# A per-pack table of planner choices, and a second side bank late, in a fused attention and GLU kernel

## The chip, the cores and the metric

One core of a Trainium2 chip runs the whole program. The metric is the device time of one execution in microseconds (us); the median of several executions is compared. A kernel is planned in Python when it is built, so on the chip every engine follows a fixed list of instructions with waits on semaphores.

The engines are called PE (matrix products; PEld is its weight load), DVE (vector), ACT (scalar, with the exp and gelu tables), POOL (GpSimd) and SP (issues DMAs).

## The reference

For x of 2048 rows and 640 columns in bf16, with 32 heads of 20 columns that share one key and one value head:

```python
q = (LN(x) @ wq) as 32 heads of 20;  k = LN(x) @ wk;  v = LN(x) @ wv
p = softmax(q k^T / sqrt(20))              # 32 x 2048 x 2048 scores
h = x + (p v, heads side by side) @ wo
g = LN(h) @ w_gate;  u = LN(h) @ w_up      # 640 -> 1536
out = h + (gelu(g) * u) @ w_down
```

LN is a layer norm without weights; gelu is the tanh form.

## The kernel before, in words

**Tiles and units.** The rows are 16 tiles of 128. The queries are taken in nine chunks (`CHUNKS`): seven of two tiles and two of one tile (tiles 14 and 15). A chunk's 32 heads make four units for two tiles, or two units for one tile; there are 32 units. Each unit meets the 16 key tiles, so there are 32 x 16 = 512 *packs*. A pack is four score matmuls of 128 x 512 in four PSUM banks (L1306), one for each row group of the PE array. `state["npack"]` counts the packs that have been issued; it is the key of every per-pack choice and ends at 512.

**Exp on two engines.** A score tile is turned into its exponential on ACT (L1688, one bank alone or two adjoining banks in one instruction) or on DVE. DVE writes an integer whose bits are a rough exponential (L1782), and two shifted copies of it refine the result; these are made by POOL (L1756 for one tile, L1738 for both shifts of one) or by DVE (L1732). A DVE tile so needs three value products on PE (L1390) where an ACT tile needs one. The value products of a unit gather in an accumulation bank, 6 or 7.

**Banks.** Scores use banks 0 to 5. Banks 6 and 7 hold the accumulation of the open unit and one side product at a time; when neither is in use they may take scores. A *side product* is any other work of PE: queries, wo, gate, up and down products, and transposes on PE. It is a `_Job` of several pieces, with a bank of its own from its first piece until another engine has emptied it (L609 while scores run, L605 afterwards).

**The planner.** A forward loop takes the engine that is free earliest, by estimated costs, and asks its function (`pe_decide`, `act_decide`, ...) for the next instruction. For PE the order is: a pack if four score banks are free; half a pack (two rows) if two are free and the estimate finds it worth while (`HALF_ON and light(t) and ...`); else value products, a piece of a side product or a filler matmul on zeros (L1529), each only if it ends before `lim`, the estimated time of the next pack. `issue_qk` chooses how many tiles of a whole pack go to DVE from DVE's backlog (usually one), and `issue_half` does so for each half. `next_piece` picks the side product and its bank: `pool_b` is [7, 6], with banks 5 and 4 while keys are being made (`head`) and all six others once all scores are issued (`tail`).

**Choices by hand.** `tw(kind, d)` looks up `TWEAK[(kind, npack)]` and otherwise returns the planner's own value `d`. Its kinds are "n" (DVE tiles of a whole pack), "a" and "b" (those of the first and the second half), "h" (split the pack or not), "l" (ns added to `lim`), "m" (no side product now) and "t" (three banks in one exp). In the kernel before `TWEAK` is empty.

**The end of the work.** `PE_T2` lists the tiles whose normalised rows of the second layer norm are transposed on PE (five transposes and a copy) rather than by a DMA of SP; `PE_TO` and `PE_ON` do so for other transposes. Gate products are emptied by DVE (L960) and go through gelu on ACT later (L987) while exps remain, and go straight through gelu (L962) after the last exp. Up products are multiplied in by DVE (L1004). The down products are added to the rows by DVE (L1022), and SP stores the tile.

Of the kernel before, what the change touches and what calls it, by code (L numbers as in the profile page):

```python
# [219 lines left out]
def bass_sequential_preLN__grouped_kv_mqa__glu_gated_geglu__prompt_kernel(  # L220
# [37 lines left out]
    PH = (8, 99)  # L258
    PE_T1 = (0, 1)
    LN_POOL = (2, 4, 6, 8)  # L260
    PE_T2 = (15,)
    PE_TO = (15,)
    PE_ON = (30, 31)
    POOL_NM = 750.0
# [94 lines left out]
    def c_act(n):  # L359
        return n / 1.2 + 51.0  # L360
# [11 lines left out]
    PVF = 99  # L372
# [15 lines left out]
    LOCKW = 200.0  # L388
    YIELD = 700.0
    WQA = 1  # L390
    TWEAK = {}
    T_LAT = (1700.0, 2700.0, 2700.0)
    ADDW = 60.0
    MISCMAX = 1500.0
# [39 lines left out]
    active = []  # L434
    sp_tasks = []
    state = {"mode": "m", "tab": "exp", "npack": 0, "exps_left": 2048, "misc_ready": False, "kv_left": NT, "qk_left": 512, "half": None}
# [28 lines left out]
    def ln_group(ln, tiles, prio, done):  # L465
# [38 lines left out]
        def norm(t):  # L504
# [9 lines left out]
            def then(op):  # L514
# [14 lines left out]

                if t in (PE_T1 if ln == 0 else PE_T2):  # L530
                    tr_job(("tr", ln, t), xn_tmp[:, s, :], ("xt", s), o, wkeys, lambda: slots["xt"].append(s),
# [83 lines left out]
    def tr_job(name, src, key, o, wkeys, sent, done):  # L615

        pieces = []
        for c in range(NC_D):
            pieces.append(((lambda c: lambda e, b, mode: e.transpose(
                psb[:, b * 1024 + c * P:b * 1024 + (c + 1) * P], src[:, c * P:(c + 1) * P], ident[:]))(c),  # L620
                "t", [key, "ident"]))

        def then(b):
            sent()

            def fin(op):
                free_bank(b)
                done(op)
            flex_copy(o, psb[:, b * 1024:b * 1024 + D].rearrange("p (c n) -> p c n", c=NC_D), D, [("b", b)], wkeys,
                      0.1, fin)  # L630
        jobs.append(_Job(name, 0.1, pieces, then))
# [481 lines left out]
    def open_units():  # L1113
        return [u for u in units if u["npk"] > 0 and not u["evac"]]

    def next_pack(t):
        nopen = 0
        for u in units:
            if u["evac"]:
                continue  # L1120
            if u["npk"] > 0:
                nopen += 1
            if u["left"]:
                if u["npk"] == 0 and nopen >= 2:
                    return None
                if u["qop"] is None or u["qop"].vis > t + 20:
                    return None
                for kt in u["left"]:
                    op = key_ready.get(kt)
                    if op is not None and op.vis <= t + 20:  # L1130
                        return u, kt
                if u["npk"] == 0:
                    return None
            if nopen >= 2:
                return None
        return None
# [18 lines left out]
    def free_banks(t):  # L1155
        res = []
        for b in score_banks():
            if bank_owner[b] is None:
                res.append((plan.ready("pe", (), [("b", b)]), b))
        return sorted(b for r, b in res if r <= t + 30), res  # L1160
# [23 lines left out]
    def tw(kind, d):  # L1184

        return TWEAK.get((kind, state["npack"]), d)

# [245 lines left out]
    def pe_decide(t):  # L1433
        half = state["half"]
        cand = half or next_pack(t)
        piece = None if tw("m", 0) else next_piece(t)
        state["misc_ready"] = piece is not None
        ok, allb = free_banks(t)
        if half is not None:
            if len(ok) >= 2:  # L1440
                issue_half(t, half[0], half[1], half[2], ok, None)
                return True
        elif cand and len(ok) >= 4:
            issue_qk(t, cand[0], cand[1], ok)
            return True

        tq = 1e12
        if cand:
            est = [x[0] for x in allb]
            ta = plan.free["act"]  # L1450
            for kind, tl in act_q:
                ta = max(ta, tl[0]["vis"]) + c_act(512 * len(tl))
                est += [ta + L_ACT] * len(tl)
            td = plan.free["dve"]
            for x in dve_q:
                td = max(td, x["vis"]) + 600
                est.append(td + L_DVE)
            est.sort()
            tq = est[3] if len(est) > 3 else 1e12
            if half is not None:  # L1460
                tq = est[1] if len(est) > 1 else 1e12
            elif len(ok) >= 2 and state["npack"] > HBEG and state["tab"] == "exp" and tw(
                    "h", HALF_ON and light(t) and tq + 445.0 - act_end() > HGAIN):
                k = state["npack"]
                state["nhalf"] = state.get("nhalf", 0) + 1
                issue_half(t, cand[0], cand[1], [k % 4, (k + 1) % 4], ok, [(k + 2) % 4, (k + 3) % 4])
                return True
        lim = max(tq, act_end() - 570.0) + tw("l", 0.0)
        qs = pv_rounds(t)
        full = min(len(q) for q in qs)  # L1470
        most = max(len(q) for q in qs)
        flush = any(u["closed"] for u in open_units())
        nr = full if not flush else most
        press = pa_free.count(True) < PRA or pd_free.count(True) < PRD
        if press and nr == 0:
            nr = min(most, 1)
        def fits(c):
            return t + c <= lim

        def do_pv():  # L1480
            sw = pe_sw(t, "v")
            k = 1
            issue_pv(t, qs, k)
            return True

        def do_piece():
            jb, pc = piece
            issue_piece(t, jb, pc)
            return True

        swv = pe_sw(t, "v")
        can_v = nr >= 1 and (fits(216.0 + swv) or press)
        can_m = piece is not None and fits(c_pe(piece[1][1], "v") + (
            pe_sw(t, "m") if piece[1][1] == "t" else swv))
        if can_v and (press or state["qk_left"] == 0):
            return do_pv()
        if can_m and piece[0].prio < 1.0:
            return do_piece()
        if can_v and nr >= PVF:
            return do_pv()  # L1500
        if can_m:
            return do_piece()
        if can_v:
            return do_pv()
        if fits(222.0 + swv) and quiet(t):
            return fill(t)
        return False
# [30 lines left out]
    def next_piece(t):  # L1538
        for jb in active:
            pc = jb.pieces[jb.pos]  # L1540
            if plan.ready("pe", pc[2], [("b", jb.bank)]) <= t + 20:
                return jb, pc
        if len(active) >= 2:
            return None
        banks = []
        need_acc = any(u["acc"] is None for u in open_units()) and not (
            state["kv_left"] == 0 and any(bank_owner[b] is not None and bank_owner[b][0] == "acc" for b in (6, 7)))
        head = state["kv_left"] > 0
        tail = state["qk_left"] == 0
        pool_b = [7, 6]  # L1550
        if head and state["npack"] < HEADN:
            pool_b += [5, 4] if state["npack"] < HEAD2 else [5]
        if tail:
            pool_b += [5, 4, 3, 2, 1, 0]
        for b in pool_b:
            if bank_owner[b] is None:
                banks.append(b)
        fixed = [b for b in banks if b in (6, 7)]
        if need_acc and len(fixed) <= 1 and fixed:
            banks = [b for b in banks if b not in (6, 7)]  # L1560
        if not banks:
            return None
        cur = min([u["id"] for u in units if u["left"]] or [99])
        best = None
        for jb in jobs:
            pr = jb.prio
            if jb.name[0] == "q":
                ahead = jb.name[1] - cur
                pr = 0.2 if ahead <= 0 else (0.9 if ahead <= 1 else 8.0 + 0.01 * ahead)
            elif jb.name[0] == "qd":  # L1570
                pr = 0.5 if jb.name[1] - cur <= QAHEAD + 1 else QPRI + 0.01 * jb.name[1]
            if best is not None and pr >= best[0]:
                continue
            if jb.gate is not None and not jb.gate():
                continue
            if any(k not in plan.w for k in jb.pieces[0][2]):
                continue
            for b in banks:
                if plan.ready("pe", jb.pieces[0][2], [("b", b)]) <= t + 20:
                    best = (pr, jb, b)  # L1580
                    break
        if best is None:
            return None
        jb = best[1]
        return _Start(jb, best[2]), jb.pieces[0]
# [311 lines left out]
    while True:  # L1897
# [6 lines left out]
        if eng in ("pe", "dve", "act"):  # L1904
# [10 lines left out]
            k = (int(t // 100000), eng, why)  # L1915
# [85 lines left out]
```

The softmax here doesn't subtract the row's maximum and nothing guards it: scores larger than these inputs give would overflow.

## Time and profile before

| what | value |
|---|---|
| median of 8 executions | 772.97 us (771.25 to 775.39) |
| profiled execution | 771.25 us, span of its instructions 769.5 us |
| mean granted clock of PE | 0.998 |
| score tiles: on DVE, on ACT | 630, 1418 |
| start of pack 25, of pack 460, of pack 511 | 55.4, 663.5, 738.7 us |
| last exp on ACT ends | 740.9 us |

Times in the tables are counted from the start of the span. A row of a group gives the line, engine, operation and shapes, the count after x, then the time that the group was busy and the mean length of one, then how long the engine had been idle before these instructions and what ended that. A wait row gives who waited for whom: the sum in us, how often, and the longest. A pack's start is that of its first score matmul, counted off in fours from the 2048 in the trace.

### The profile page before, as it was taken

The numbers are of one execution on the slowest core, as the hardware profiler recorded it, in microseconds if no ns is written. First come the engines' busy times: TensorE is split into PE (matmuls) and PEld (weight loads), VectorE is DVE, ScalarE is ACT, GpSimd is POOL, SyncE is SP. The second block draws the span as 40 slices with busy tenths as digits, with TensorE's granted clock in tenths as the row PEclk, the third lists the DMA queues.
The fourth block names the chain that finished last, engine by engine and source line by source line (L and its number), as shares of the span: only waits on it lengthen the run. The fifth ranks groups of instructions, "written<-read, shape, count | busy, mean of one in ns | idle before, by whom it ended". The sixth has DMA issues, their size and how long they took to land.

```text
span 769.5 us, 29575 instructions
## 1 busy us (share of the span) xinstructions
PE 710.3 (92%) x12946; PEld 336.0 (44%) x12946; DVE 611.7 (80%) x1113; ACT 726.2 (94%) x1086; POOL 659.7 (86%) x721
## 2 busy tenths in 40 slices
PE   4788899999889899999999899999899999989998
PEld 3332223342334455445334444455444544434567
DVE  8878888888988767878788777878788786888853
ACT  5899999999999999999999999999999999999961
POOL 5698998999999888989999987879898998998740
PEclk9999999999999999999999999999999999999999
DMA  7543421000110001100101001010011000211000
GB/s 209 97 126 86 109 62 26 20 9 9 26 26 9 10 12 35 26 26 10 24 11 26 3 10 44 9 43 10 4 35 35 9 10 12 35 26 18 12 19 19
DMA packets 56768, 25.88 MB, mean 34 GB/s; under 512 B 47808, under 2 KB 55360, under 8 KB 56640
## 3 DMA queue, kind: packets, MB, share of 16 engines
q1 hardware_dynamic: 55328, 23.55, 13.5%
q8 instruction: 103, 1.69, 0.9%
q10 hardware_dynamic: 1312, 0.44, 0.2%
q14 instruction: 25, 0.20, 0.1%
HBM read 10.21 MB, written 2.62 MB: 17 GB/s over the span
## 4 chain that ended last, share of the span: by engine, by line
PE 55%; ACT 32%; DVE 8%; DMA 3%; issue 1%; POOL 0%; DVEq 0%
ACT pa L1688 31%; PE ps L609 21%; PE ps L1390 16%; PE ps L1306 14%; DVE pd L1782 5%; PE ps L605 3%; DMA xn1T<-xn_tmp 1%; DVE osb L1417 1%; DMA xh<-in_A_x_dram 1%; ACT gbuf L987 1%; PE ps L1529 1%; DVE gbuf L1004 1%; DMA onr<-osb 1%; DVE qT L679 0%; ACT L1688 0%
## 5 line engine op out<-in xcount | busy, mean ns | idle before, releaser
L1688 ACT ACTIVATE pa<-ps 128x512 bf16<-128x512 f32 (+1 forms) x1038 | 680.6, 815 | 12.0 <-PE ps L1306 6.7
L1756 POOL TENSOR_TENSOR pd<-pd,shifts 128x512 int32<-128x512 int32 x564 | 574.7, 1040 | 64.9 <-DVE pd L1782 60.5
L1782 DVE TENSOR_SCALAR pd<-ps 128x512 uint16<-128x512 f32 x630 | 417.8, 687 | 121.1 <-PE ps L1306 111.0
L1390 PE MATMUL ps<-pd,v_ext 128*32 128x512 bf16 x1890 | 291.2, 383 | 13.8 <-DVE osb L1417 7.0
L1390 PE MATMUL ps<-pa,v_ext 128*32 128x512 bf16 x1418 | 265.9, 384 | 2.8 <-ACT pa L1688 1.7
L1306 PE MATMUL ps<-qT,kT 32*128 32x512 bf16 x2048 | 221.7, 384 | 27.7 <-DVE pd L1782 10.6
L1306 PEld LDWEIGHTS ps<-qT,kT 32*128 32x128 bf16 x2048 | 61.2, 91 | 201.5 <-DVE pd L1782 107.6
L1390 PEld LDWEIGHTS ps<-pd,v_ext 128*32 128x32 bf16 x1890 | 80.4, 95 | 78.0 <-issue 41.9
L1390 PEld LDWEIGHTS ps<-pa,v_ext 128*32 128x32 bf16 x1418 | 71.0, 95 | 41.8 <-issue 27.2
L609 PE MATMUL ps<-xn2T,wu_sb 128*32 128x256 bf16 x1680 | 67.0, 274 | 2.1 <-DVE qT L679 1.4
L609 PE MATMUL ps<-xn2T,wg_sb 128*32 128x256 bf16 x1680 | 66.3, 274 | 0.0
L609 PE MATMUL ps<-wd_sb,gbuf 128*32 128x320 bf16 x1264 | 59.2, 301 | 0.0
L609 PE MATMUL ps<-xn1T,wq_pad 128*32 128x256 bf16 (+1 forms) x1440 | 52.2, 266 | 0.7 <-ACT pa L1688 0.6
L609 PEld LDWEIGHTS ps<-xn2T,wu_sb 128*32 128x32 bf16 x1680 | 42.9, 96 | 20.2 <-issue 9.7
L609 PEld LDWEIGHTS ps<-xn2T,wg_sb 128*32 128x32 bf16 x1680 | 41.5, 96 | 18.5 <-issue 12.0
L1738 POOL TENSOR_TENSOR pd<-pd,shifts 128x256 int32<-128x256 int32 x64 | 42.8, 687 | 0.0
L609 PEld LDWEIGHTS ps<-wd_sb,gbuf 128*32 128x32 bf16 x1264 | 31.6, 96 | 20.9 <-issue 9.7
L1004 DVE TENSOR_TENSOR gbuf<-ps,gbuf 128x512 bf16<-128x512 f32 x48 | 32.9, 685 | 9.6 <-PE ps L605 5.0
L609 PEld LDWEIGHTS ps<-xn1T,wq_pad 128*32 128x32 bf16 x1440 | 33.5, 97 | 14.5 <-issue 8.4
L462 DVE BATCH_NORM_STATS2 stats<-xh 128x6 f32<-128x320 bf16 x64 | 29.9, 476 | 1.5 <-DMA xh<-in_A_x_dram 1.0
L609 PE MATMUL ps<-wo_sb,onT 128*32 128x320 bf16 x600 | 29.7, 301 | 0.0
L960 DVE CAST gbuf<-ps 128x512 bf16<-128x512 f32 x42 | 28.8, 686 | 0.3
(76 smaller groups left out, 355.1 us busy)
## 6 DMA issues: line engine op xcount, KB each, us to landing
out_dram<-xh SPq DMA_DIRECT2D x16, 160.0 KB, 1.8
xh<-in_A_x_dram SPq DMA_DIRECT2D x3, 640.0 KB, 6.5
wd_sb<-in_B_w_down_dram SPq DMA_DIRECT2D x4, 480.0 KB, 3.7
wg_sb<-in_B_w_gate_dram SPq DMA_DIRECT2D x2, 576.0 KB, 5.3
wu_sb<-in_B_w_up_dram SPq DMA_DIRECT2D x2, 576.0 KB, 5.6
wg_sb<-in_B_w_gate_dram SPq DMA_DIRECT2D x2, 384.0 KB, 4.1
wu_sb<-in_B_w_up_dram SPq DMA_DIRECT2D x2, 384.0 KB, 4.4
wo_sb<-in_A_wo_dram SPq DMA_DIRECT2D x1, 480.0 KB, 3.5
```

The source lines that it names most:

```text
L462: dve(lambda e: e.bn_stats(stats[:, ln, t, 6 * h:6 * h + 6], xh[:, t, h * HALF:(h + 1) * HALF]), 395, [key], [("st", ln, t, h)], prio, c)
L605: return e.matmul(o(b), l, r, start=st, stop=sp)
L609: ins = e.matmul(o(b)[a, :], l[:, a], r, start=st, stop=sp, tile_position=(0, 32 * j))
L960: dve(lambda e: e.tensor_copy(o, i), c_dve(n * k), [("b", bk)], ks, 1.0, fin)
L987: task(("act",), (lambda v: lambda e: e.activation(v, v, ACT.Gelu_apprx_tanh))(v), ("gelu", c_act(n * (f1 - f0))), L_ACT, ks, ks, 1.0, (la ...
L1004: dve(lambda e: e.tensor_tensor(o, i, o, ALU.mult), c_dve(n * k), [("b", bk)] + ks, ks, 1.0, fin)
L1306: ins = e.matmul(bank(b), kT4[32 * r:32 * r + 32, kt * P:(kt + 1) * P], qT[32 * r:32 * r + 32, s, :], start=True, stop=True, tile_position ...
L1390: ins = e.matmul(ps[32 * r:32 * r + 32, ab * 512:(ab + 1) * 512], v_ext[:, it["kt"], it["w"], :], it["ap"], start=st, stop=(j in ends), ti ...
L1688: op = plan.commit("act", lambda e: e.activation(dst, src, ACT.Exp, scale=SM_SCALE), cost, L_ACT, [("b", b0 + db * i) for i in range(n)], ...
L1738: return e.tensor_tensor(pd32[:, w, h], pd32[:, 0, h], shifts[:, w - 1:w].to_broadcast([P, 256 * k]), ALU.add)
L1756: return e.tensor_tensor(pd32[:, 1:3, h], pd32[:, 0, h].unsqueeze(1).to_broadcast([P, 2, 256 * k]), shifts[:].unsqueeze(2).to_broadcast([P ...
L1782: op = plan.commit("dve", lambda e: e.tensor_scalar(pd[:, 0, s * 512:(s + 1) * 512], bank(b), CH_A, CH_B, ALU.mult, ALU.add), c_dve(512), ...
```

## The change

Four things change. `TWEAK` is filled from a table with 132 entries, by kind and pack number. A new kind "v" lets value products go ahead of side products in a pack. From pack 460 on, and while fewer than two side products are active, a side product may take bank 5 as well as 6 and 7. And the second layer norm of tile 14, not of tile 15 alone, is transposed on PE. The branch with `PVF` was not reached before, since `PVF` is 99; `next_piece` returned nothing before too when two side products were active, so `LACT = 2` sets no further limit.

```diff
-    PE_T2 = (15,)
+    PE_T2 = (14, 15)
...
-    TWEAK = {}
+
+    TABLE = {
+        "a": {27: 1, 28: 1, 44: 1, 127: 1, 140: 0, 142: 0, 171: 0, 295: 1, 369: 1, 379: 0, 434: 1, 441: 1,
+             464: 1},
+        "b": {29: 0, 78: 1, 96: 0, 125: 0, 203: 1, 301: 0, 345: 0, 395: 1, 426: 1, 428: 1, 432: 0, 446: 1,
+             504: 1, 523: 0},
+        "h": {42: 1, 72: 0, 80: 0, 95: 1, 115: 1, 194: 0, 215: 0, 223: 0, 236: 1, 270: 1, 283: 1, 287: 1,
+             324: 0, 347: 0, 349: 1, 350: 0, 358: 1, 374: 1, 382: 0, 432: 0, 467: 0, 471: 1},
+        "l": {26: -200.0, 35: 150.0, 98: -200.0, 106: -100.0, 124: -200.0, 131: 150.0, 136: 300.0, 158: 300.0,
+             208: 150.0, 211: -400.0, 221: -200.0, 240: 300.0, 272: 300.0, 280: -200.0, 294: 300.0, 304: 150.0,
+             308: -200.0, 310: -100.0, 333: -100.0, 335: -100.0, 346: 300.0, 368: -100.0, 370: -200.0,
+             395: -400.0, 408: -200.0, 409: 300.0, 423: -100.0, 439: 300.0, 449: -200.0, 477: 300.0,
+             479: -200.0, 482: 150.0, 484: 150.0, 488: -100.0, 495: 150.0, 506: -100.0, 511: 150.0,
+             526: -400.0},
+        "m": {107: 1, 119: 1, 305: 1, 335: 1, 449: 1, 519: 1},
+        "n": {27: 0, 35: 2, 72: 2, 137: 2, 176: 1, 195: 1, 207: 1, 244: 0, 287: 1, 326: 1, 347: 1, 366: 1,
+             408: 1, 417: 2, 441: 1, 447: 0, 478: 2, 487: 1, 511: 0, 518: 0, 523: 1, 525: 0},
+        "v": {25: 1, 33: 1, 90: 1, 138: 1, 139: 1, 142: 1, 155: 1, 192: 1, 210: 1, 253: 1, 256: 1, 281: 1,
+             358: 1, 359: 1, 505: 1, 514: 1, 519: 1},
+    }
+    TWEAK = {(kind, k): v for kind, row in TABLE.items() for k, v in row.items()}
+    LATE = 460
+    LACT = 2
...
-        if can_v and nr >= PVF:
+        if can_v and (nr >= PVF or tw("v", 0)):
             return do_pv()
...
         if tail:
             pool_b += [5, 4, 3, 2, 1, 0]
+        elif state["npack"] >= LATE and len(active) < LACT:
+            pool_b += [5]
```

## The prediction

> **What bounds the kernel now.** I read the engine shares first, then the busy time by stretch, then the groups of instructions, the waits of the score stage, and the order of instructions at the end.
>
> ```profile
> PE 710.3 (92%) x12946; PEld 336.0 (44%) x12946; DVE 611.7 (80%) x1113; ACT 726.2 (94%) x1086; POOL 659.7 (86%) x721
> ```
> ```profile
> 0.00:60.00 60.00, 43.70 (x776) 20.32 (x776) 48.12 (x142) 47.16 (x75) 44.78 (x82) 0.97 0.59 141
> 60.00:740.00 680.00, 639.96 (x11834) 293.48 (x11831) 552.19 (x948) 671.88 (x1004) 613.35 (x639) 1.00 0.11 25
> 740.00:769.50 29.50, 26.64 (x346) 22.22 (x343) 11.43 (x24) 7.19 (x10) 1.57 (x2) 1.00 0.07 24
> ```
>
> The columns after the length are PE, PEld, DVE, ACT, POOL. In the 680 us of the score stage ACT is busy 671.88 us, so 8.1 us are left to it; DVE has 127.8 us and POOL 66.7 us idle. ACT sets the rate there. PE looks full, but it runs 324 filler matmuls on the zero tile (28.7 us), which the planner issues only when PE has been slack.
>
> ```profile
> L1756 POOL TENSOR_TENSOR pd<-pd,shifts 128x512 int32<-128x512 int32 x564 | 574.7, 1040 | 64.9 <-DVE pd L1782 60.5 <-DVE ln_ve L480 0.4 <-DVE ln_vb L480 0.4
> L1782 DVE TENSOR_SCALAR pd<-ps 128x512 uint16<-128x512 f32 x630 | 417.8, 687 | 121.1 <-PE ps L1306 111.0
> L1688 ACT ACTIVATE pa<-ps 128x1024 bf16<-128x1024 f32 x380 | 407.3, 1078 | 2.3 <-PE ps L1306 2.0
> L1688 ACT ACTIVATE pa<-ps 128x512 bf16<-128x512 f32 x658 | 390.7, 664 | 9.8 <-PE ps L1306 4.7
> ```
>
> Of 2048 score tiles 630 go to DVE (1.23 per pack of four) and 1418 to ACT, 760 in pairs and 658 alone. The means include an overlap with the next instruction: the median distance between starts of back-to-back ones is 904 ns for a pair, 478 ns for a single and 607 ns for a DVE tile. These spacings are the prices below.
>
> ```profile
> DVE pd L1782 <- PE ps L1306: 105.4, 179, 1.2
> PEld ps L1306 <- DVE pd L1782: 104.0, 304, 1.1
> PEld ps L1306 <- ACT pa L1688: 48.7, 109, 0.9
> ACT pa L1688 <- PE ps L1306: 2.8, 13, 0.4
> ```
>
> These waits are of 60 to 740 us. Scores wait for banks that ACT and DVE must empty; DVE waits for scores; ACT waits for almost nothing.
>
> At the end the chain is another. The last exp ends at 740.9, and the order of instructions shows:
>
> ```profile
> 741.80 0.69 DVE L1417 CAST osb<-ps 128x512 bf16<-128x512 f32 x1 [1.91 <-PE ps L1390]
> ...
> 752.35 0.71 ACT L678 ACTIVATE xn2T<-ps 128x640 bf16<-128x640 bf16 x1 [0.80 <-PE ps L619]
> ...
> 754.32 3.14 PEld L605 LDWEIGHTS ps<-wd_sb,gbuf 128*128 128x128 bf16 x24
> 754.38 3.42 PE L605 MATMUL ps<-wd_sb,gbuf 128*128 128x320 bf16 x24
> ...
> 766.68 0.49 DVE L1022 TENSOR_TENSOR xh<-xh,ps 128x320 bf16<-128x320 bf16 x1 [1.14 <-PE ps L605]
> ```
>
> From 741.8 to 753.1 the last unit is normalised and tile 15 goes through wo and LN2, while PE does what is left of tile 13 (20 down matmuls) and tile 14's gates and ups; after 753.1 comes tile 15's own MLP, with tile 14's 24 down matmuls (3.42 us) in between.
>
> [...]a bank lent to a side product is lost to scores until it is emptied; the scores' waits for DVE and ACT above agree. [...]The trace has 1283 ns each time[...]: a load at 430.84 is followed by its gelu at 432.13. I use 1283. [...]DVE's shifted copies (L1732) take 354 to 1160 ns[...], but there are 36 of them; the added tiles are mostly finished by POOL.
>
> **The change part by part.** The first 25 packs are untouched: the smallest key is 25, and that pack's scores start at 55.4 us. Of 132 entries 8 have keys of 514 or more; there are 512 packs, so they are never read. An "n" is read only where a pack is issued whole, "a" and "b" only where it is split, so more are inert.
>
> *Tiles moved ("n", "a", "b").* Live "n": five 2s, ten 1s, four 0s. With 1.23 tiles per pack a 1 mostly restates the choice, so +5-4 = +1 at most in sum. "a": nine 1s, four 0s, +5. "b": seven 1s and six live 0s, +1. Together +7 tiles if every entry turned a choice; I take +5. A tile from ACT to DVE turns a pair and a single (1382 ns) into two singles (956), or a pair (904) into a single (478): 426 ns of ACT each. So 5 x 0.426 = 2.1 us less. It costs DVE 607 ns, POOL 1040 ns and two more value products; 5 tiles need 3 and 5 us of the idle 128 and 67. If that cover is gone, POOL at 1.04 us a tile becomes the limit after some 60 tiles. The heuristic reads DVE's backlog again at each pack, so the sum can drift: between 5 tiles lost (+2) and 25 gained (-10.7).
>
> *Order ("h", "l", "m", "v"; 22, 37, 5 and 15 live entries).* They add no instruction. A split lets two rows start when two banks are free, "l" moves by -400 to +300 ns the time up to which PE may start other work, "m" keeps side products out for a pack, "v" puts value products first. At best they return ACT's 8.1 us; at worst they put scores behind later PE work: the 17 positive "l" entries add up to 3.9 us, +4. I take half of the idle time: -4.0.
>
> *Second side bank from pack 460.* That pack starts at 663.5 us, so 52 packs over 75 us. Now some 20 side products pass through one bank there (240 gate, 240 up, 120 wo, 112 down matmuls), and tile 14, whose transpose was issued at 717.6 and landed 3.5 us later, has its first gate at 744.9. With bank 5 too, tile 13's downs and tile 14's MLP can run before the scores end. The most it saves is the 3.42 us of tile 14's downs and about 1 us ahead of tile 15's chain: -4.4. But a gate emptied while exps remain goes through DVE and a gelu on ACT: two loads and 1.39 us, 2 x 1.28 + 1.39 = 3.95 us on the bounding engine. And with five score banks a pack can need the previous pair's banks: then ACT sits for the wait (0.23 us) and from score start to first reader (702.16 to 702.61, 0.45), 0.68 us a pack. Ends: -4.4, and +15 (below). I take -1.0.
>
> *Tile 14's transpose on PE.* One DMA of SP's queue and its 3.5 us go; five transposes (0.44 us) and a copy (0.71 on ACT, 0.60 on DVE) come, and a side bank is held. The DMA was not waited for (24 us of slack), so 0; if ACT gets the copy, +0.7, and if the gates come forward, up to 2 us earlier. What stood behind that DMA on SP is output stores, not late.
>
> Sum: -2.1 - 4.0 - 1.0 + 0 = -7.1, say -7. The profiled execution took 771.25 us, 1.75 beyond its span and 1.7 below the median of 772.97. So 764.2 for such an execution and **766.0** as a median. About 0.2% (1.5 us) is what a measurement of this kernel can tell from no change.
>
> **The rivals.**
> 1. *Bank 5 starves ACT (slower).* If ten of the 20 side products use it for about 3 us each, that is 30 us or 22 packs at 0.68 us, +15; against it the tail's -4.4 and the table's -6. Net +4.6: 777.6. For: scores already wait 153 us for banks. Against: splits restart with two banks, and DVE idles enough to empty more. It decides from 10.4/0.68 = 15 packs.
> 2. *The table shifts no ACT work.* The idle time of 8.1 us is spread over some thousand instructions, and what one entry closes opens elsewhere; net 0, 773.0. For: half or more of the "n" entries restate the usual choice. Against: ACT's spacings are so regular that an order laid out ahead should hold.
> 3. *A large gain.* Small shifts keep DVE's backlog low, so the heuristic gives it 25 more tiles (-10.7), 6 us of idle time go and the tail gives 3: -20, 753. For: DVE's 128 us. Against: POOL would rise by 26 us, to 94% of the stage.
>
> **How the numbers follow.** Forecast (gain of 2 to 13) 0.56, large gain 0.15, no change 0.10, starved ACT 0.19. So faster 0.71, same 0.10, slower 0.19. The forecast's own range is 760 to 771; reaching to the rivals gives 755 to 777.
>
> **What would show it.** Right: DVE tiles at 633 to 640, ACT's idle time in the score stage near 4 us, the last exp at 734 to 737, tile 14's first gate before it, and 25 to 28 us from there to the end of the span (28.6 now). Wrong: "ACT waits for scores" far over 2.8 us, most of it after 663 us (rival 1); 630 tiles and 8 us idle as before (rival 2); over 650 tiles (rival 3). A span that shortens while ACT's busy time does not fall would disprove the tiles' term; two more table loads before the last exp would show the gelu's price paid.

## The result, and the profile after

The changed kernel takes 766.73 us (median of 11 executions, 763.20 to 769.97) against 772.55 for the kernel before (median of 32): -5.8 us, ratio 0.9926 with a 95% interval of 0.9912 to 0.9941. The forecast was 766.0.

The engine shares of the page after:

```profile
PE 713.9 (93%) x12972; PEld 334.9 (44%) x12972; DVE 616.7 (80%) x1117; ACT 724.2 (94%) x1084; POOL 658.9 (86%) x724
PEclk9999999999999999998999999999999999999999
```

Hardly anything moved between engines. The second line is the one to stop at: the tensor clock in 40 slices has a slice of 8 in the middle of the score stage, which the page before didn't have. The busy time by stretch (columns PE, PEld, DVE, ACT, POOL, then the clock):

```profile
60.00:740.00 680.00, 647.09 (x11817) 294.23 (x11813) 558.80 (x956) 669.33 (x1002) 613.78 (x644) 0.99 0.12 25
740.00:767.00 27.00, 24.16 (x405) 20.34 (x397) 10.87 (x23) 8.77 (x12) 1.43 (x2) 0.99 0.06 20
```

ACT's idle time in 60 to 740 us is 10.7 us, where the forecast had some 4 and the kernel before 8.1. The groups of instructions by shape (count, then busy us and mean ns):

```profile
L1806 DVE TENSOR_SCALAR pd<-ps 128x512 uint16<-128x512 f32 x631 | 419.1, 687 | 114.5 <-PE ps L1328 105.6
L1712 ACT ACTIVATE pa<-ps 128x1024 bf16<-128x1024 f32 x381 | 414.3, 1091 | 4.2 <-PE ps L1328 3.3 <-PE ps L1412 0.9
L1712 ACT ACTIVATE pa<-ps 128x512 bf16<-128x512 f32 x655 | 393.6, 672 | 11.4 <-PE ps L1328 6.6 <-PE ps L1412 0.8
```

631 DVE tiles against 630: in the end the whole change moved one tile, not five. That is not the table's doing. The same groups in the kernel with the table alone, one of the experiments below:

```profile
L1806 DVE TENSOR_SCALAR pd<-ps 128x512 uint16<-128x512 f32 x636 | 422.1, 687 | 111.4 <-PE ps L1328 102.6
L1712 ACT ACTIVATE pa<-ps 128x1024 bf16<-128x1024 f32 x378 | 410.1, 1088 | 3.1 <-PE ps L1328 3.1
L1712 ACT ACTIVATE pa<-ps 128x512 bf16<-128x512 f32 x656 | 393.0, 672 | 10.7 <-PE ps L1328 5.6 <-PE ps L1412 0.8
```

There 636 tiles are on DVE, six more than before. By the start of pack 490 the changed kernel and the table alone have each begun 610 tiles on DVE, and the kernel before 603. Five go back to ACT between there and pack 511, after bank 5 has been lent.

**The profiled execution shows less than the median.** It took 768.79 us (span 767.0), at a mean clock of 0.991. The same program was profiled again, below, at 0.998: span 763.2. Both have 3.41 us at half speed at some 26 us, and the clock records of the first have a second such stretch, of 10.24 us from 357.0 us on. A mean of 0.998 is called full clock from here on: in every profile at that mean the only stretch at half speed, up to the last us or two of the span, is one of 3.41 us that begins in the first 30 us. By stretch of time, first the execution with the fall, then the one at full clock:

```profile
340.00:360.00 20.00, 18.95 (x308) 8.21 (x304) 15.95 (x26) 18.81 (x29) 18.42 (x19) 0.92 0.04 9
360.00:380.00 20.00, 20.00 (x270) 7.28 (x268) 13.84 (x24) 17.11 (x27) 16.27 (x19) 0.82 0.01 2
```
```profile
340.00:360.00 20.00, 18.94 (x335) 8.77 (x328) 16.71 (x27) 19.46 (x32) 18.96 (x20) 1.00 0.04 9
360.00:380.00 20.00, 19.49 (x299) 7.66 (x297) 16.95 (x28) 20.00 (x33) 19.34 (x23) 1.00 0.05 9
```

PE is "busier" with the fall (38.95 us of 40 instead of 38.43) and everything else does less: ACT 35.9 us of work in 40 instead of 39.5, DVE 29.8 instead of 33.7, POOL 34.7 instead of 38.3. The score matmuls in the order of instructions of the first:

```profile
353.59 0.39 PE L1328 MATMUL ps<-qT,kT 32*128 32x512 bf16 x4
...
356.13 0.39 PE L1328 MATMUL ps<-qT,kT 32*128 32x512 bf16 x2
...
358.57 0.61 PE L1328 MATMUL ps<-qT,kT 32*128 32x512 bf16 x2
```

A group of score matmuls that took 0.39 us takes 0.61 after 357.0. From pack 25 to pack 250 the two executions of one program need 310.7 and 306.2 us: the fall costs 4.5 us. (The table alone, with the same order up to pack 490, has a fall of 6.83 us from 356.9 on in its profile and needs 309.2 us: 3.0 more.)

**A ledger at full clock.** Pack starts are counted from the score matmuls of the two traces (kernel before; the changed one at clock 0.998).

| stretch | before | after, full clock | difference |
|---|---|---|---|
| start to pack 25 (the order is the same) | 55.4 | 57.2 | +1.8 |
| pack 25 to pack 511 | 683.3 | 679.2 | -4.1 |
| pack 511 to end of span | 30.7 | 26.8 | -3.9 |

The first row is chance: in the profiles of the experiments below, pack 25 starts at 55.3 to 57.5 us after the same instructions. So the change is worth some 8 us at full clock. Over all executions whose mean clock was 0.998 the medians are 771.41 (21 of the kernel before, as the runs below list them) and 763.48 (five of the changed kernel): -7.9.

### The profile page after: what moved, and what is told of

Read it like the earlier page. It is cut to its first block, busy times and chain, and to the rows that moved or that the text cites. A ratio compares the mean times of both kernels' runs of the same rounds, so it can differ in the third digit from the quotient of the medians.

```text
span 767.0 us, 29623 instructions
## 1 busy us (share of the span) xinstructions
PE 713.9 (93%) x12972; PEld 334.9 (44%) x12972; DVE 616.7 (80%) x1117; ACT 724.2 (94%) x1084; POOL 658.9 (86%) x724
## 4 chain that ended last, share of the span: by engine, by line
PE 55%; ACT 32%; DVE 7%; POOL 2%; DMA 2%; issue 1%; SPq 0%
ACT pa L1712 30%; PE ps L631 21%; PE ps L1412 16%; PE ps L1328 15%; DVE pd L1806 4%; PE ps L627 3%; POOL pd L1780 2%; ACT gbuf L1009 1%; DMA xn1T<-xn_tmp 1%; DVE pd L1756 1%; DMA wv_sb<-in_A_wv_dram 1%; PE ps L1551 1%; DVE osb L1439 1%; ACT L1712 1%; ACT L1009 1%
## 5 line engine op out<-in xcount | busy, mean ns | idle before, releaser
L1412 PE MATMUL ps<-pa,v_ext 128*32 128x512 bf16 x1417 | 256.6, 386 | 2.7 <-DVE osb L1439 0.8
L1328 PE MATMUL ps<-qT,kT 32*128 32x512 bf16 x2048 | 226.2, 386 | 28.3 <-DVE pd L1806 13.4
L1412 PEld LDWEIGHTS ps<-pa,v_ext 128*32 128x32 bf16 x1417 | 68.1, 95 | 42.1 <-issue 26.3
L631 PE MATMUL ps<-xn2T,wg_sb 128*32 128x256 bf16 (+1 forms) x1764 | 68.1, 271 | 0.1
L631 PE MATMUL ps<-wd_sb,gbuf 128*32 128x320 bf16 x1344 | 63.5, 301 | 0.1
L631 PE MATMUL ps<-xn1T,wq_pad 128*32 128x256 bf16 (+1 forms) x1440 | 55.0, 270 | 0.8 <-ACT pa L1712 0.6
L631 PEld LDWEIGHTS ps<-xn2T,wg_sb 128*32 128x32 bf16 x1764 | 43.4, 96 | 18.8 <-issue 12.1
L1762 POOL TENSOR_TENSOR pd<-pd,shifts 128x256 int32<-128x256 int32 x73 | 47.7, 672 | 0.0
L484 DVE BATCH_NORM_STATS2 stats<-xh 128x6 f32<-128x320 bf16 x64 | 29.8, 476 | 1.3 <-DMA xh<-in_A_x_dram 1.1
```

The lines of the kernel that those rows point to most:

```text
L484: dve(lambda e: e.bn_stats(stats[:, ln, t, 6 * h:6 * h + 6], xh[:, t, h * HALF:(h + 1) * HALF]), 395, [key], [("st", ln, t, h)], prio, c)
L631: ins = e.matmul(o(b)[a, :], l[:, a], r, start=st, stop=sp, tile_position=(0, 32 * j))
L1328: ins = e.matmul(bank(b), kT4[32 * r:32 * r + 32, kt * P:(kt + 1) * P], qT[32 * r:32 * r + 32, s, :], start=True, stop=True, tile_position ...
L1412: ins = e.matmul(ps[32 * r:32 * r + 32, ab * 512:(ab + 1) * 512], v_ext[:, it["kt"], it["w"], :], it["ap"], start=st, stop=(j in ends), ti ...
L1762: return e.tensor_tensor(pd32[:, w, h], pd32[:, 0, h], shifts[:, w - 1:w].to_broadcast([P, 256 * k]), ALU.add)
```

## The experiments

Each is timed against the kernel before on its own chip. "Tail" is the time from the end of the last exp to the end of the span.

### The same program again

No edit.

> The changed kernel once more, as the yardstick of its neighbours. Its executions so far lie between 763.2 and 770.0 us and go with the mean granted clock (0.998 to 0.989). Theory A ([...]one or more stretches at half clock in a sparse place of the score stage): the lowest executions, about 763 us, have a mean clock of 0.998, and 0.007 less of mean clock goes with 5 us more. Theory B (the spread comes from elsewhere and the clock only follows): a profile at a clock of 0.998 shows no shorter score stage than one at 0.991.

Measured: 764.79 us, ratio 0.9918 (0.9894 to 0.9941). The three executions at clock 0.998 took 763.5 to 765.0 us, one at 0.989 took 769.3. Theory A holds: with one program, a profile at full clock has the shorter score stage.

The tail in this profile, in order of time:

```profile
735.27 3.54 ACT L1712 ACTIVATE pa<-ps 128x512 bf16<-128x512 f32 x4
...
737.17 0.28 PE L631 MATMUL ps<-xn2T,wg_sb 128*32 128x128 bf16 x2
...
739.30 0.69 DVE L1439 CAST osb<-ps 128x512 bf16<-128x512 f32 x1 [2.75 <-PE ps L1412]
740.12 1.09 ACT L984 ACTIVATE gbuf<-ps 128x512 bf16<-128x512 f32 x2
...
748.62 1.79 PE L627 MATMUL ps<-wd_sb,gbuf 128*128 128x320 bf16 x12
748.82 0.70 ACT L700 ACTIVATE xn2T<-ps 128x640 bf16<-128x640 bf16 x1 [2.54 <-PE ps L641]
```

Tile 14's gate products begin at 737.17, before the last exp ends at 738.81, where the kernel before came to them 4 us after it. But they are emptied after it (740.12, straight through gelu), so no DVE copy and no change of table is paid in the score stage. Of tile 14 only 12 down matmuls (1.79 us) stand behind tile 15's transposed rows; before it was 24 and 20 ups.

### The table alone, and the late bank without the table

```diff
-    PE_T2 = (14, 15)          # table alone
+    PE_T2 = (15,)
-    LATE = 460
+    LATE = 9999
```
```diff
-    TWEAK = {... for kind, row in TABLE.items() ...}    # without the table
+    TWEAK = {... for kind, row in TABLE.items() ... if kind in ""}    # empty
```

> The table alone: no bank 5 late, tile 15 alone transposed on PE. By the prediction's sum the table is worth 6 of the 7 us: 767 to 768, with the tail from last exp to end of span as before (28.6 us). Rival (the late bank is the gain, since the tail is what got shorter in the changed kernel's profile): 771 to 773.

> Bank 5 from pack 460 and tile 14's transpose on PE, without the table. By the prediction's sum -1: 771 to 772, with a tail shorter by up to 4.4 us and the score stage longer by up to 4. Rival (the tail's 4 us are the gain): 768 to 769. Rival 1 of the prediction (bank 5 starves ACT): 775 or more.

Measured: the table alone 767.76 us, ratio 0.9953 (0.9935 to 0.9971), tail 28.1 us; at clock 0.998, four executions of 766.05 to 766.76. Without the table 770.34 us, ratio 0.9981 (0.9973 to 0.9989), tail 28.4 us. The table alone gives what was expected of it, in time and in tiles (six moved; 5.0 us at full clock, 766.3 against 771.3). Without the table the late bank and tile 14's transpose together give 1.9 us and none of the tail's 4, so the rival that the tail gains without the table is out. At full clock it is 1.2 us (770.1 against 771.3), and the profile has 1.1 us less between pack 460 and 511 (74.1 us against 75.2); which of the two edits brings that wasn't separated. In this kernel the planner never lends bank 5 while scores remain, so the gain isn't a loan's doing directly, and the run says nothing of rival 1; the run with bank 5 open from pack 60 does.

### The table and the late bank, without tile 14's transpose on PE

```diff
-    PE_T2 = (14, 15)
+    PE_T2 = (15,)
```

> The table and bank 5 from pack 460, but tile 15 alone transposed on PE. In the order that the planner writes here, as in the changed kernel, bank 5 is lent once in all after pack 460, to an up product at pack 490; without the table it is never lent. Theory A (the single loan moves the side work ahead and so takes the tail's 4 us; tile 14's transpose counts for nothing): 764 to 767, tail 24 to 25 us. Theory B (tile 14's transpose on PE is what lets its gates begin early): about 768, tail 28 us as with the table alone.

Measured: 764.25 us, ratio 0.9897 (0.9883 to 0.9911), tail 24.7 us, three of four executions at 0.998 with 763.28 to 764.75. Theory A holds: tile 14's transpose on PE counts for nothing that shows. Against the table alone, at 0.998, the late bank is worth 2.5 us (766.3 to 763.8). DVE runs the same instructions in the same order in the changed kernel and with the table alone up to 706 us, where pack 490 is. So one loan of a bank there, and what the planner orders differently after it, ends the down products of tiles 12 and 13 at 736.0, 2.8 us before the last exp, and not at 742.7, 3.0 us after it. It has a price too: of the six tiles that the table moves to DVE one or two are left (636 tiles with the table alone, 632 here, 631 in the changed kernel), and the stretch from pack 460 to 511 takes 73.1 and 73.5 us where the table alone takes 72.5. How much is the loan itself and how much the order that follows wasn't separated.

The tail of the table alone:

```profile
740.19 2.48 PE L627 MATMUL ps<-wd_sb,gbuf 128*128 128x320 bf16 x17
740.29 0.69 DVE L1439 CAST osb<-ps 128x512 bf16<-128x512 f32 x1 [2.62 <-PE ps L1412]
...
742.73 2.40 PE L627 MATMUL ps<-xn2T,wg_sb 128*128 128x128 bf16 x40
...
753.43 0.70 ACT L700 ACTIVATE xn2T<-ps 128x640 bf16<-128x640 bf16 x1 [2.68 <-PE ps L641]
```

Down products still run at 740.19 and tile 14's gates start 3 us after the last exp (739.67). Tile 15's transposed rows come 13.8 us after the last exp; with the late bank it is 10.0.

### Bank 5 open from pack 60

```diff
-    LATE = 460
+    LATE = 60
-    TWEAK = {... for kind, row in TABLE.items() ...}
+    TWEAK = {... for kind, row in TABLE.items() ... if kind in ""}    # empty
```

> No table, and bank 5 open to side products from pack 60 rather than 460 (tile 14 on PE as well). The planner then lends it 18 times in the score stage instead of never. The prediction's first rival prices a loan at some two packs of 0.68 us, so 18 loans 24 us: 796 at most, less where packs are split. If a loan costs ACT nothing: 770 to 772. Half price: about 783.

Measured: 783.49 us, ratio 1.0143 (1.0126 to 1.0159), last exp at 753.2, tail 28.4. The wait that the first rival named, in the waits of 60 to 740 us:

```profile
ACT pa L1712 <- PE ps L1328: 15.8, 34, 0.8
```

It was 2.8 us in the kernel before. So lent banks do starve ACT, at about half the price put on them: 11.6 us for 18 loans, 0.64 us each, against the kernel before. Against the run above with the late bank and no loan, which by its median was 1.9 us faster than the kernel before, it is some 13 us or 0.7 each. The order around a loan changes too, so this is not the price of the loan alone. The rival's mechanism is real; the change lends once.

### Half of the table at a time

```diff
-    TWEAK = {... for kind, row in TABLE.items() for k, v in row.items()}
+    TWEAK = {... for kind, row in TABLE.items() for k, v in row.items() if kind in "nab"}     # or "hlmv"
     # both: LATE = 9999, PE_T2 = (15,)
```

> Only the entries that choose counts of DVE tiles (n, a, b), no late bank, tile 15 alone on PE. By the prediction -2.1 us and some 635 DVE tiles: 770. Rival (the entries fit one course of the planner and lose their sense when others are missing): 772 to 778, whatever the count of tiles.

> Only the entries that shift order (h, l, m, v), no late bank, tile 15 alone on PE. By the prediction -4 us: 768. Rival (one course only): 772 to 775; then the two halves of the table together give less than nothing, and the whole table's 4.4 us are not a sum over entries.

Measured: tiles alone 774.42 us, ratio 1.0028 (1.0017 to 1.0039), with 634 DVE tiles; order alone 772.26 us, ratio 0.9999 (0.9991 to 1.0008), with 632. Alone the halves lose 2.3 and gain 0; together they gain 4.4. The prediction costed them as a sum, and in time they aren't one. In tiles they are: +4 and +2, and +6 for the whole table. More tiles on DVE (+4) did not make the first half faster.

### Every key one pack later

```diff
-    TWEAK = {(kind, k): v ...}
+    TWEAK = {(kind, k + 1): v ...}
```

> The changed kernel with every key of the table raised by one: the same entries, each applied one pack later; late bank and tile 14's transpose as in the change. If the entries are good in kind (more tiles here, more room there), most of the gain stays: 765 to 769. If each is a correction to one exact course of the planner, the gain is gone: 772 to 780.

Measured: 778.03 us, ratio 1.0072 (1.0059 to 1.0086), last exp at 746.2 us: 6.1 us slower than the kernel before, which has no table at all. So the entries aren't good in kind. They belong to one exact course of the planner, which answers each shift with another order of all that follows. Some do nothing at all: with all 14 "b" entries taken out, the order on all five engines is the same to the last instruction.

### Filler matmuls and the clock

In the first, four matmuls on zeros go ahead of a step of value products wherever PE is under 60% busy by the plan; in the second only in packs 241 to 250. In the third and fourth the fillers that the planner itself set are cut short. The order is that of the changed kernel (in the last, of the kernel before).

```diff
+            if warm_up:                    # 115 steps; second kernel: five
+                for r in range(4):
+                    e.matmul(ps[..., ab0 * 512:(ab0 + 1) * 512], zz[:], kT4[:, 0:512], start=False, stop=False, ...)
             for j, (r, ab, it, st, u) in enumerate(calls):
```
```diff
-  e.matmul(ps[..., ab * 512:ab * 512 + n * P], zz[:], kT4[:, 0:n * P], ...)     # fill(), cut short
+  e.matmul(ps[..., ab * 512:ab * 512 + 32], zz[:], kT4[:, 0:32], ...)
```

> The changed kernel with the same order on every engine, and four filler matmuls of 512 columns on the zero tile ahead of a step of value products wherever the planner's own account has PE under 60% busy over the last 3.4 us (115 places, 0.216 us of PE each, most of it in slack). Theory A[...]: no stretch at half clock after the first 30 us, the executions close up, median about 763 to 764. Theory B (the clock only follows): spread and median stay, or the fillers' PE time makes it slower, 767 to 770.

> The changed kernel with the same order, and five filler steps (four matmuls of 512 columns on zeros) ahead of value products in packs 241 to 250 alone, the sparse place in which the profiled execution fell to half clock for 10.2 us. Clock theory: the fall at 357 us goes, mean clock 0.998, executions close up at 763 to 765; the fillers' own price by the run with 115 of them (16 us more) is 5 x 0.14 = 0.7 us. If the fall has another cause, or five are too few: clock 0.989 to 0.998 and 766 to 767 as before.

> The changed kernel with the same order, its 55 filler steps cut from 512 columns to 32, so that they occupy PE for almost no time. Clock theory: PE falls to half clock more often, mean clock 0.98 or less, and the time rises by 0.5 to 0.7 us for each 0.001 of clock, to 770 or more. Rival (fillers only cost): clock as before and faster by some of the 0.2 to 0.4 us a step, 755 to 763.

> The kernel before with its 81 filler steps cut from 512 columns to 32, order unchanged. Clock theory: it owes its even executions (clock 0.995 to 1.0) to the fillers, so the clock falls to 0.98 or less and the time rises to 778 or more. Rival (fillers only cost): 760 to 770 at the same clock.

| kernel | median us | ratio (95%) | mean clock of its executions |
|---|---|---|---|
| 115 fillers more | 780.74 | 1.0113 (1.0096 to 1.0130) | 0.995 to 1.000 |
| five fillers more | 766.28 | 0.9922 (0.9908 to 0.9935) | 0.995 to 0.998 |
| changed, fillers short | 766.86 | 0.9932 (0.9916 to 0.9947) | 0.984 to 0.991 |
| before, fillers short | 776.67 | 1.0055 (1.0042 to 1.0069) | 0.982 to 0.987 |

With 115 fillers the profile has no stretch at half speed after 31 us, and the kernel loses some 15 us: ACT waits 11.6 us for scores in 60 to 740 us, where it waited 3.1 at full clock in the changed kernel. The idle time of PE here is not free, since a pack's scores go out the moment that four banks are free, and a filler step of 0.22 us (the spacing of such groups in the trace) then stands in front. The expected 0.216 us "in slack" was wrong.

With five fillers the place is at full clock in the profile, and no execution is under 0.995:

```profile
340.00:360.00 20.00, 18.94 (x319) 8.01 (x311) 15.97 (x26) 19.10 (x31) 18.79 (x19) 1.00 0.04 9
360.00:380.00 20.00, 19.45 (x299) 7.62 (x300) 16.41 (x28) 19.97 (x32) 18.76 (x22) 1.00 0.04 9
```

That fits the theory and doesn't prove it. Without these fillers the changed kernel had seven under 0.995 among the twelve executions listed for its first run, but one of six in its second, and the table with the late bank none of four. The executions close up (764.7 to 767.7), but the median is not better: at clock 0.998 it needs 765.6 and 765.8, some 2 us more than the changed kernel. If the fillers do prevent the fall, they cost about what they save.

Cutting the planner's own fillers lowers the mean clock in both kernels, as the clock theory has it: to 0.984 to 0.991 from 0.989 to 0.998 in the changed one, and to 0.982 to 0.987 from 0.995 to 1.000 in the kernel before. The kernel before pays 4.8 us for it: its profile has 17.07 us at half speed in the first 60 us, and two falls of 3.41 us at 260.8 and 407.6, and needs 685.9 us from pack 25 to 511, where it was 683.3. The changed one ends where it was, against the 770 expected. Its profile, at a mean of 0.991, has 13.65 us at half speed in the first 60 us and no fall at 357 or elsewhere in the score stage, and takes 765.24 us, where the first profile at the same mean took 768.79. So it matters where a fall lies, and the mean clock alone doesn't tell the time. From pack 25 to 511 it needs 679.4 us, as with the fillers (679.2): in the changed order they had no price that shows. No version here beats the changed kernel clearly: table and late bank without tile 14's transpose has the lowest median (764.25), but only four executions, none of them with a long fall of the clock, and at 0.998 the two are the same.

## Why the prediction was right, and where

**What bounds the kernel: right.** ACT stays at its rate (7.0 us idle of 680 at full clock, where it was 8.1); both gains are in its stage and in the tail.

**The tiles' term (-2.1): right for the table, and then taken back.** The table by itself moves six tiles, and ACT has two pairs and two singles fewer: 2 x 0.904 + 2 x 0.478 = 2.8 us less. That all "b" entries are inert was not foreseen, and the count came out all the same. In the whole change one tile is left: ACT's work falls by three singles and rises by one pair, 0.904 - 3 x 0.478 = -0.5 us. What failed is the adding up of the four terms, as if the late bank left the table's tiles where they were. And the "n", "a" and "b" entries alone made the kernel slower, so tiles moved were not a gain by themselves.

**The order's term (-4.0): right in direction, somewhat too large.** Adding up, over all exps after 60 us, the distance from start to next start less 478 or 904 ns, and leaving out the gelus and table loads, gives 28.5 us of lost time before and 25.3 after at full clock: -3.2. With the -0.5 of work that is -3.7 of the -4.1 us between packs 25 and 511. For the table alone, 681.3 us less the 3.0 of its fall is 5.0 under the kernel before; less the 2.8 of work, 2.2 are left for the order. Half of the idle time was a choice, not a reading, so that the size is near is luck; that order and counts are worth nothing apart was not foreseen. Rival 2 (no ACT time won) is refuted by the table alone.

**The late bank (-1.0): right mechanism, wrong size.** On top of the table it is worth 2.5 us. The tail's end of the bound (-4.4) was nearly reached, -4.1, and most of the costs set against it did not come: tile 14's gates were emptied after the last exp, so the 3.95 us of gelu and table loads (1283 ns a load in the traces of both kernels) were never in the score stage, and bank 5 was lent once, not for ten products. Starving was priced at twice what the loans from pack 60 on cost (some 1.4 us a loan against 0.64 to 0.7), and rival 1's 30 us are some 20 packs of 1.47 us, not 22, which takes 1 us off its 15. The cost that did come, five tiles back on ACT, was not on the list.

**Tile 14's transpose (0): right.** Taking it out of the whole change left 764.25 us.

**What was missing: the clock.** The prediction called the fillers a sign of slack and costed no consequence of having fewer. The changed order sets 55 filler steps where the order before set 81, and in the execution with the fall PE is busy for 3.06 of the 4 us from 353 to 357, after 12.89 of the 13 before them. That this is why the clock falls there is argued, not shown: with its fillers cut the changed order did not fall there in its profile. What the falls cost is measured. The median execution of the changed kernel is 3.2 us over its full-clock time (766.73 against 763.48), that of the kernel before 1.1 (772.55 against 771.41). So at full clock -0.5 of work, -3.2 of lost time, -0.4 left over and -3.9 after pack 511 make -8.0, by the medians -7.9; +2.1 of clock makes the -5.8 measured. That the total of -7 came near is luck in part: the bank's term was too small, and the clock's was absent.

**The signs named beforehand.** Tile 14's early gate came. The DVE tiles (633 to 640; it was 631), ACT's idle time (near 4 us; it was 10.7, and 7.0 at full clock), the last exp (734 to 737; it was 742.6, and 738.8 at full clock) and the tail (25 to 28 us; it was 24.4) missed.

## What to carry to other kernels

Where instructions are ordered ahead by a greedy planner, costing a table of overrides entry by entry tells little of the time: halves of it, or the whole of it one step late, gave +0 to +6 us where the whole gave -4.4, although the tiles moved came out as counted. Terms of one change also act on each other: one bank lent at pack 490 won some 3.5 us at the end and gave back five of the tiles that the table had moved. Judge such a table by what it leaves on the bounding engine and by the tail, and tie it to the exact planner that it was made for. And a plan's estimated costs don't contain the granted clock: look at the clock row of several executions before believing one profile.

## What the runs showed of the hardware that was not expected

PE's clock falls to half, in the clock records of these traces, for 3.41, 6.83, 10.24, 13.65 or 17.07 us at a time (of the stretches that end before the span does): one to five times 3.41 us. In the first profile 327.68 us, 96.0 times 3.41, lie between the end of the first stretch and the start of the second.

PE does not stand still before the falls of the first profile: it was busy for 2.59 of the 3.41 us before the one at 357.0, and for 1.89 of the 3.41 us before the one at 25.9. Nor does thin use decide alone. The longest pause of PE from 349 to 357 us, 0.80 us that ends at 354.79, stands in the execution at full clock too, where it ends at 355.48; PE's busy time from 340 to 360 us is 18.95 us in the one and 18.94 in the other. And the kernel before has PE busy for 2.78 of the 3.40 us from 373.0 on, with no fall after it. What sets off a fall stays open, and so does why one program has the fall in some executions and not in others (mean clock 0.989 to 0.998, 763.2 to 770.0 us).

A fall in the score stage cost 4.5 us for 10.24 us and 3.0 for 6.83; one of 13.65 us in the first 60 us, where ACT is busy for some 45 us, left no mark on the span (763.4 us, the changed kernel with its fillers cut).
